# Sooner loads and a new order of scores in a windowed-attention and ReGLU kernel

## The chip, the cores and the metric

The kernel runs on one core of one Trainium2 chip. The metric is device time in microseconds, as the median of several executions, each kernel beside executions of the kernel before on the same chip in the same rounds. The profile of a kernel is one traced execution; its span, from the first to the last instruction of the core, is 1.7 to 1.8 us shorter than the device time of the same execution.

## The reference

Attention over q, k, v of shape (4, 8, 768, 64), in which a row sees the first 4 positions and its last 128; the output, as 3072 rows of 512, goes through a gated feed-forward layer.

```python
keep = is_sink | in_window                 # n_sink = 4, window = 128
a = softmax(where(keep, q @ k.T / sqrt(64), -1e9))
x = (a @ v).transpose(0, 2, 1, 3).reshape(3072, 512)
out = (maximum(x @ w_gate, 0) * (x @ w_val)) @ w_out      # d_ff = 1536
```

## The kernel before

Attention works in 16 units: unit i is one pair of heads of batch i // 4, so the "first four pairs" are batch 0. The feed-forward work is cut into 96 chunks, each half a batch (384 rows) by 128 of the 1536 columns. Units 0 to 3 and the first three stages of unit 4 run first; after them the stages of attention are put between chunks by a plan.

A unit's k, q and v are loaded from DRAM into f32 staging (four buffers in turn) by the SP queue. GpSimd casts them to bf16 and issues the weight loads on its own queue. In batches 0 and 1 TensorE transposes q and k (`T`); in batches 2 and 3 a DMA on the SP queue does (`X`). VectorE then copies strips of kT into kTs (`sinkk`).

```python
def X(self):                      # batches 2 and 3: two transposes by DMA, on the SP queue
    for x, dst in ((self.kn, kT[self.s]), (self.qn, qT[self.s])):
        nc.sync.dma_start_transpose(...)

def held(x):                      # a load that waits for VectorE to reach this memset
    if x < len(U):
        nc.vector.memset(U[x].stg[0:1, 0:1], 0.0)
        load(x)                   # k, q, v0, v1 on nc.sync; vt too for a batch's first unit

def unit_stages(x):
    u, prev, nxt = U[x], at(x - 1), at(x + 1)
    def s(gi):                    # scores of group gi, then exp on ScalarE
        def f():
            # ... cut
            if gi == 0 and nxt is not None and nxt.xbar:
                nxt.X()
            u.S(gi)
        return f
    def v():                      # second outputs of the unit before, and their normalisation
        if prev is not None:
            norm(prev, 1, ps_at if on_array else ps_gv)
    def t():                      # next unit's T and kTs, then loads, casts, weights
        # ... cut: nxt.T(...), nxt.sinkk()
        if x == 3:
            load(6)
        elif x == 4:
            load(7)
        elif x >= 5:
            held(x + 3)
        # ... cut: load_wo at x = 4 and 5; casts(at(x + 3), "kqv"); load_w at x = 0, 1, 3, 4
        if x == 0:
            load(5)
    # ... cut: v0 is norm(u, 0)
    if x < NP:
        return [s(0), v, s(1), t, s(2), v0]

def chunk(b, c0, n, m):           # cut to its operations
    gp = x @ wg[:, m]             # four matmuls on TensorE, PSUM pool of three buffers
    gs = relu(gp)                 # ScalarE
    vp = x @ wv[:, m]             # four matmuls, same pool
    hT[:, m] = gs * vp            # VectorE
PLAN = ((0, 28), (24, 50), (48, 62), (71, 74))    # (chunk, stages to be out by then)
```

The softmax here doesn't subtract the row's maximum and nothing guards it: scores larger than these inputs give would overflow.

## Time and profile before

| | before |
|---|---|
| device time | 260.46 us (259.57 to 260.71, 3 runs) |
| span of the traced run | 258.7 us |
| TensorE busy | 249.4 us, 96% |
| TensorE's last long wait | 1.97 us, for hT, to 75.87 |
| span from there to the end | 182.8 us |

Most lines behind it are in the prediction below; the one on which TensorE resumes is

```profile
75.87 0.81 PE L290 MATMUL gp<-xT,wg 128*128 128x384 bf16 x4 [1.97 <-DVE hT L298]
```

A timeline line is start, duration, engine, source line, operation, output <- inputs, shapes, count; the bracket tells how long the engine stood idle before it and what ended that.

### The profile page before, as it was taken

The numbers are of one execution on the slowest core, as the hardware profiler recorded it, in microseconds if no ns is written. First come the engines' busy times: TensorE is split into PE (matmuls) and PEld (weight loads), VectorE is DVE, ScalarE is ACT, GpSimd is POOL, SyncE is SP. The second block draws the span as 40 slices with busy tenths as digits, with TensorE's granted clock in tenths as the row PEclk, the third lists the DMA queues.
The fourth block names the chain that finished last, engine by engine and source line by source line (L and its number), as shares of the span: only waits on it lengthen the run. The fifth ranks groups of instructions, "written<-read, shape, count | busy, mean of one in ns | idle before, by whom it ended". The sixth has DMA issues, their size and how long they took to land.

```text
span 258.7 us, 5201 instructions
## 1 busy us (share of the span) xinstructions
PE 249.4 (96%) x2046; PEld 143.5 (55%) x2046; DVE 144.5 (56%) x313; ACT 115.6 (45%) x188; POOL 62.3 (24%) x94
## 2 busy tenths in 40 slices
PE   7999799999969999999999999999999999999994
PEld 7565466565545555546555555556555555555443
DVE  2598869886748564756656665756664322322100
ACT  3887665647424444443535344344533332333212
POOL 6779538801535221404040210000000000000000
PEclk9999999999999999999999999999999999999999
DMA  7999999999989948869491961311011101111132
GB/s 213 309 279 253 246 257 197 196 198 199 218 125 239 197 111 157 129 145 138 85 242 43 184 104 42 61 43 41 3 41 41 42 1 41 43 41 41 41 112 94
DMA packets 77320, 33.56 MB, mean 130 GB/s; under 512 B 64368, under 2 KB 74352, under 8 KB 77296
## 3 DMA queue, kind: packets, MB, share of 16 engines
q1 hardware_dynamic: 69920, 28.12, 48.5%
q0 software_dynamic: 5808, 4.72, 12.1%
q10 hardware_dynamic: 1568, 0.39, 0.7%
q8 instruction: 16, 0.26, 0.5%
q14 instruction: 8, 0.07, 0.1%
HBM read 28.51 MB, written 6.29 MB: 135 GB/s over the span
## 4 chain that ended last, share of the span: by engine, by line
PE 68%; DMA 13%; SPq 8%; POOL 6%; issue 2%; DVE 1%; ACT 0%; POOLq 0%; DVEq 0%; ACTq 0%
PE op L310 23%; PE gp L290 19%; PE vp L296 18%; DMA stg<-in_v_dram 11%; PE ops L206 5%; SPq L119 4%; PE sps L181 3%; SPq L114 2%; DMA kT<-kn 2%; POOL vn L129 2%; SPq L111 1%; SPq L331 1%; POOL kn L126 1%; POOL vn L130 1%; POOL wg L225 1%
## 5 line engine op out<-in xcount | busy, mean ns | idle before, releaser
L298 DVE TENSOR_TENSOR hT<-gs,vp 128x384 bf16<-128x384 f32 x96 | 52.8, 550 | 54.4 <-PE vp L296 52.7
L290 PE MATMUL gp<-xT,wg 128*128 128x384 bf16 x384 | 78.5, 327 | 2.0 <-DVE hT L298 2.0
L296 PE MATMUL vp<-xT,wv 128*128 128x384 bf16 x384 | 78.1, 326 | 1.1 <-DMA wv<-in_moe_w_val_dram 1.1
L293 ACT ACTIVATE gs<-gp 128x384 f32<-128x384 f32 x96 | 47.1, 490 | 61.5 <-PE gp L290 60.3
L310 PE MATMUL op<-wo,hT 128*128 128x512 bf16 (+1 forms) x300 | 74.4, 370 | 0.0
L185 ACT ACTIVATE ee<-sps 128x1006 bf16<-128x1006 f32 (+2 forms) x48 | 46.1, 966 | 46.9 <-PE sps L181 46.8
L296 PEld LDWEIGHTS <-wv 128*128 128x128 bf16 x384 | 37.5, 98 | 26.2 <-DMA wv<-in_moe_w_val_dram 1.5
L290 PEld LDWEIGHTS <-wg 128*128 128x128 bf16 x384 | 34.0, 98 | 31.8 <-issue 6.7
L310 PEld LDWEIGHTS <-hT 128*128 128x128 bf16 x300 | 29.4, 98 | 25.0
L187 DVE TENSOR_TENSOR ee<-ee,msk 128x1006 bf16<-128x1006 bf16 (+2 forms) x36 | 25.1, 698 | 11.3 <-ACT ee L185 11.3
L126 POOL CAST kn<-stg 128x768 bf16<-128x768 f32 x15 | 13.2, 879 | 59.0 <-DMA stg<-in_k_dram 39.6
L314 ACT COPY ot<-op 128x512 f32<-128x512 f32 (+1 forms) x25 | 14.2, 569 | 24.5 <-PE op L310 24.5
L275 DVE STREAM_TRANSPOSE R<-ops 128x384 f32<-128x384 f32 x24 | 13.9, 581 | 12.6 <-PE ops L206 12.5
L278 DVE STREAM_TRANSPOSE R<-rc 128x384 f32<-128x384 f32 x32 | 18.5, 578 | 1.1
L280 DVE TENSOR_TENSOR xT<-ops,R 128x384 bf16<-128x384 f32 x32 | 17.8, 557 | 1.7
L206 PEld LDWEIGHTS <-ones 128*64 128x64 bf16 x288 | 12.3, 109 | 11.2 <-issue 10.8
L129 POOL CAST vn<-stg 128x768 bf16<-128x768 f32 x16 | 13.3, 832 | 15.0 <-DMA stg<-in_v_dram 15.0
L126 POOL CAST qn<-stg 128x768 bf16<-128x768 f32 x15 | 13.3, 888 | 11.9 <-DMA stg<-in_q_dram 7.1
L206 PE MATMUL ops<-ee,vn 128*64 128x255 bf16 (+7 forms) x256 | 15.3, 240 | 0.2 <-DVE xT L280 0.2
L181 PE MATMUL sps<-qT,kT 64*128 64x251 bf16 (+2 forms) x128 | 14.7, 252 | 0.5 <-ACT qT L154 0.4
L181 PEld LDWEIGHTS <-kT 64*128 64x128 bf16 x128 | 6.3, 93 | 12.9 <-issue 10.5
L181 PE MATMUL sps<-qT,kTs 64*128 64x248 bf16 (+1 forms) x96 | 12.3, 253 | 0.0
(57 smaller groups left out, 135.5 us busy)
## 6 DMA issues: line engine op xcount, KB each, us to landing
stg<-in_k_dram SPq DMA_DIRECT2D x16, 384.0 KB, 4.9
stg<-in_q_dram SPq DMA_DIRECT2D x16, 384.0 KB, 5.4
out_dram<-ot SPq DMA_DIRECT2D x23, 256.0 KB, 2.0
stg<-in_v_dram SPq DMA_DIRECT2D x30, 192.0 KB, 5.4
wg<-in_moe_w_gate_dram POOLq DMA_DIRECT2D x4, 384.0 KB, 7.7
wv<-in_moe_w_val_dram POOLq DMA_DIRECT2D x4, 384.0 KB, 9.8
wo<-in_moe_w_out_dram POOLq DMA_DIRECT2D x3, 512.0 KB, 13.6
stg<-in_v_dram ACTq DMA_DIRECT2D x2, 192.0 KB, 6.4
```

The source lines that it names most:

```text
L126: cp((self.kn if what == "k" else self.qn)[:], self.staging(what).rearrange("p h (n d) -> p n h d", d=64))
L129: eng.tensor_copy(self.vn[:], self.staging("v"))
L181: nc.tensor.matmul(out=ps[:, h, c:c + w], lhsT=self.kw(j, r), rhs=qT[s][r, qa:qa + w], start=not self.biased, stop=True, skip_group_check= ...
L185: nc.scalar.activation(x, ps[:, :, 0:c], Act.Exp, bias=0.0, scale=scale)
L187: nc.vector.tensor_tensor(x, x, bc(msk[:, m0:m0 + c], 2), op=Alu.mult)
L206: nc.tensor.matmul(out=ps[1 - what][64 * h:64 * h + 64, qa - q0:qa - q0 + w], lhsT=self.vw(j, h) if what else ones[:], rhs=ee[s][:, gi, h, ...
L278: nc.vector.transpose(r[:, 1, 0:w], bass.AP(a.tensor, a.offset, [a.ap[0], [1, nb], [0, 32]]))
L290: nc.tensor.matmul(out=gp[:, 0:n], lhsT=wg[:, ko, m * 128:(m + 1) * 128], rhs=x[:, ko, c0:c0 + n], start=ko == 0, stop=ko == KO - 1)
L293: nc.scalar.activation(gs[:, 0:n], gp[:, 0:n], Act.Relu, bias=0.0, scale=1.0)
L296: nc.tensor.matmul(out=vp[:, 0:n], lhsT=wv[:, ko, m * 128:(m + 1) * 128], rhs=x[:, ko, c0:c0 + n], start=ko == 0, stop=ko == KO - 1)
L298: nc.vector.tensor_tensor(hT[:, m, c0:c0 + n], gs[:, 0:n], vp[:, 0:n], op=Alu.mult)
L310: nc.tensor.matmul(out=op, lhsT=hTs[b][:, m, t * 128:(t + 1) * 128], rhs=wo[:, m, c0:c0 + n], start=m == 0, stop=m == FM - 1)
```

## The change

The intent: ScalarE should get its second scores sooner in the first four pairs; loads of later batches should start sooner and fill a gap of the DMA engines at 42 to 47 us. (The change's description also speaks of moving w_out ahead; no line of the diff does that.)

```diff
-                if x == 3:
+                if x == 2:
+                    held(5)
+                elif x == 3:
                     load(6)
                 elif x == 4:
                     load(7)
-                elif x >= 5:
-                    held(x + 3)
+                if x >= 4:
+                    held(x + 4)
...
-                if x == 0:
-                    load(5)
...
             if x < NP:
-                return [s(0), v, s(1), t, s(2), v0]
+                return [s(0), s(1), v, t, s(2), v0]
...
-        PLAN = ((0, 28), (24, 50), (48, 62), (71, 74))
+        PLAN = ((0, 28), (6, 32), (24, 50), (48, 62), (71, 74))
```

## The prediction

> **What bounds the kernel now.** I read the page first, then who made TensorE wait, then the timeline round the largest wait, then the DMA queue's own timeline and the packets of each queue by stretch.
>
> The page: busy TensorE, the 40 slices of PE and of DMA (a slice is 6.5 us).
>
> ```profile
> PE 249.4 (96%) x2046; PEld 143.5 (55%) x2046; DVE 144.5 (56%) x313; ACT 115.6 (45%) x188; POOL 62.3 (24%) x94
> PE   7999799999969999999999999999999999999994
> DMA  7999999999989948869491961311011101111132
> ```
>
> TensorE is the bound: after its dip in slice 11 (71 to 78 us) it never stops. But the DMA engines are full for the first 71 us too, and the dips of PE lie there. TensorE's waits by releaser (us in total, times, longest):
>
> ```profile
> PE gp L290 <- DVE hT L298: 2.0, 1, 2.0
> PE vp L296 <- DMA wv<-in_moe_w_val_dram: 1.1, 1, 1.1
> ```
>
> The 2.0 us wait is at 73.9 to 75.87. VectorE's timeline there:
>
> ```profile
> 69.40 0.54 DVE L298 TENSOR_TENSOR hT<-gs,vp 128x384 bf16<-128x384 f32 x1
> 74.87 0.41 DVE L161 COPY kTs<-kT 128x372 bf16<-128x372 bf16 x1 [4.93 <-DMA kT<-kn]
> 75.27 0.54 DVE L298 TENSOR_TENSOR hT<-gs,vp 128x384 bf16<-128x384 f32 x1
> ```
>
> VectorE stands 4.93 us at kTs of unit 8 (batch 2's first pair, first to be transposed by DMA); the hT products behind it wait too, PSUM fills, and TensorE stops 2.0 us. TensorE resumes 1.0 us after kT lands (74.84 to 75.87). From there it has no stop but the tail, so the end time is: landing of unit 8's kT, plus 1.0, plus 182.8 of span (258.66 - 75.87).
>
> Why it lands at 74.8, from the DMA queue's timeline (start, time the queue's sequencer was held):
>
> ```profile
> 39.18 0.60 SPq L331 DMA_DIRECT2D vt<-in_v_dram  x1
> 47.18 0.37 SPq L111 DMA_DIRECT2D stg<-in_k_dram  x1
> 47.65 3.26 SPq L111 DMA_DIRECT2D stg<-in_q_dram  x1
> 51.01 12.26 SPq L119 DMA_DIRECT2D stg<-in_v_dram  x2
> 63.35 2.67 SPq L111 DMA_DIRECT2D stg<-in_k_dram  x1
> 66.12 1.25 SPq L111 DMA_DIRECT2D stg<-in_q_dram  x1
> 67.46 2.21 SPq L119 DMA_DIRECT2D stg<-in_v_dram  x2
> 69.84 1.62 SPq L135 DMA_TRANSPOSE kT<-kn  x1
> ```
>
> Unit 8's loads go out at 47.18 (held until then by a VectorE memset), unit 9's at 63.35, and only behind them, in program order, unit 8's transpose. The v loads hold the queue 12 us. Packets of the two queues in 50 to 65 us (first two lines) and of the load queue alone in 66 to 71 us:
>
> ```profile
> q0 software_dynamic: 2365, 2.08, 85.8%
> q1 hardware_dynamic: 3400, 0.86, 36.9%
> ```
> ```profile
> q1 hardware_dynamic: 4153, 1.05, 97.3%
> ```
>
> q0 is the weights, q1 all loads, transposes and stores of the SP queue. With both at work q1 gets 3400/15 = 227 packets per us and q0 2365/15 = 158; alone, q1 gets 4153/5 = 830. And in 42 to 47, where unit 8's loads are held back (last columns: DMA share, GB/s):
>
> ```profile
> 42.00:47.00 5.00, 5.00 (x45) 2.94 (x44) 4.79 (x10) 3.51 (x6) 5.00 (x7) 1.00 0.99 120
> 50.00:65.00 15.00, 15.00 (x137) 8.61 (x137) 11.56 (x25) 9.00 (x15) 1.86 (x2) 1.00 1.23 197
> ```
>
> That gap is what sooner loads can use.
>
> [...] in 58 to 64 us the two queues moved 927 and 925 packets, one for one, and unit 8's transpose ran only behind unit 9's loads. [...] batch 2's loads are 256 B pieces, and they ran at 210 GB/s in 66 to 71 us against 330 in 38 to 40, where unit 7's k and q came in rows of 384 f32, 1536 B. [...]
>
> **The change part by part.**
>
> (1) Order in the first four pairs. Now TensorE runs first scores, previous pair's second outputs, second scores. ScalarE waits 0.84 us per pair for the second scores (25 us: exp at 24.93), and the outputs wait some 0.3 us for the third exp. Putting scores first feeds ScalarE earlier and removes both. But the normalisation of those outputs then starts later, and the pair's own outputs need its PSUM buffer (three in that pool). VectorE needs about 2.1 us (24.11 to 26.22). The new loop is normalisation 2.1 + outputs 0.4 + two biased scores 0.85 each + sums 0.35 + hand-overs 0.35 = 4.9 us, and the pairs now take 4.9 (first scores at 21.98 and about 26.9). So nothing in the middle pairs; at the end of the stage about 0.5 us, for unit 4's scores no longer wait for qT. Then the first vp waits for wv anyway. An earlier TensorE before 70 us is in any case eaten by the wait at 74.
>
> (2) Unit 5's load moves from pair 0 to pair 2, behind a memset: its k goes out at about 22.3, not 19.39. The first weights, issued at 21.25, lose a competitor: perhaps 0.8 us off the 1.1 us wait. The load queue runs dry for about 1.2 us, some of which the weights use; I carry +0.6 us to everything behind it.
>
> (3) Loads 8 and later go out one unit sooner. Unit 8's k then follows vt directly (about 40 us). But the order on the SP queue, which I compared instruction for instruction, becomes loads 8, 9, 10, then transpose 8; before it was 8, 9, transpose 8. A unit is 128x12 + 128x12 + 2 x 128x6 = 4608 packets (check: 43 to 72 us has 9443, two units and vt). So q1 must move 13824 packets before the transpose instead of 9216. It starts at 43, not at about 50. q0's 3696 packets of 43 to 72 us take 3696/158 = 23.4 us beside it, to 66.4; q1 moves 23.4 x 227 = 5310 meanwhile; the other 8514 take 8514/830 = 10.3 us: unit 10's last packet at about 76.7. Unit 9's was at about 72.0 before (by counting). That is +4.7. The weights alone reached 215 per us in 44 to 50 (1287 in 6) only after a slow start, so q1 can take more at first: -0.8. With (2): 4.7 - 0.8 + 0.6 = +4.5 us on kT's landing, 79.3, and TensorE resumes at 80.4.
>
> (4) The added point in the plan moves stages by at most one chunk between chunks 3 and 10: nothing. The diff holds no line that moves w_out; POOL's order is unchanged, and w_out now competes with unit 8. It should land about 1 us later (before: at most 66 us; first used after 70), no wait.
>
> Later units keep their distances: load x+4 is followed by transpose x+2 as load x+3 by x+2 before, and the profile shows no wait for a transpose after the first. No new wait there. One 59 ns memset more.
>
> Sum: 260.46 + 4.5 = 265.0. I put in a fifth of a chance that the order on the queue costs less than I think, and say 264.5.
>
> **Rivals.** (a) The intended one: the loads were only late, the gap of 42 to 47 is used, unit 8 lands before 70, both waits go: 260.5 - 2.0 - up to 0.8 = about 258. For it: 120 GB/s in that gap, 4.9 us of waiting. Against it: unit 8's loads need not be the limit, the transpose's place behind a third unit is. (b) Mine: 262.5 to 267. (c) DMA work only changes places: the gap's extra packets (7 us x 227 = 1590) pay a third of the added 4608, and the rest is small if q1 beside q0 runs faster than 227; at 400 the landing moves by about +2: 262.5. (d) The weights suffer: w2 is issued at 42.03 and used at about 52.9; its 1024 packets at 158 take 6.5 us, so it lands near 51 to 52. A wait of 1 us there would be swallowed by the one at 74.
>
> **Range and chances.** Faster by over 2% means under 255.3, less than any removed wait allows: 3%. The 2% line upward is 265.7, inside my spread of 262.5 to 267.5: 37%. Within 2%: 60%. The range, 259 to 267.5, leaves (a) just outside.
>
> **What would show it.** Right: on the SP queue the transpose of unit 8 after three loads, at about 74; VectorE's wait at kTs of some 9 us ending near 79; TensorE's one wait for hT there of 6 to 7 us; the first vp's wait smaller; no gap at 42 to 47. Wrong: kTs without a wait and transpose 8 out before 68 (then (a)), or TensorE waiting for wg or wv of the later weight parts, or a wait after 90 us.

## More of the kernel before

All runs quoted here are of the state called fast.

One row of the page the prediction doesn't show will matter: the clock that was granted to TensorE, in tenths (9 is full) for 40 slices of the span.

```profile
PEclk9999999999999999999999999999999999999999
```

It is full all along in this execution. Such a row is easily passed over where nothing stands in it. It is not full in every execution of this kernel: in 11 of the 36 that ran beside the experiments the mean granted clock was 0.986 to 0.993. A mean of 0.993 stands for some 3.6 us at half clock, an estimate (0.007 x 259 us, doubled).

## The result, and the profile after

The changed kernel took 267.62 us (266.37 to 268.27, 4 runs) where the kernel before took 260.58 (259.57 to 261.67, 4 runs): ratio 1.0263, 95% interval 1.0207 to 1.0320. A second measurement later, on another chip, gave 265.78 (265.39 to 266.85, 6 runs) and 1.0202 (1.0162 to 1.0242). A ratio is the mean time of one kernel's fast runs over that of the other's fast runs of the same rounds, so not quite the ratio of the medians. So it is slower by about 5 to 7 us, on or a little over the 2% line.

TensorE's waits in the changed kernel (total, times, longest, in us):

```profile
PE gp L290 <- DVE hT L298: 5.6, 1, 5.6
PE vp L296 <- DMA wv<-in_moe_w_val_dram: 2.8, 2, 1.5
```

The one wait for hT has grown from 2.0 to 5.6 us, and there are two waits for wv. The SP queue's timeline:

```profile
41.09 1.47 SPq L111 DMA_DIRECT2D stg<-in_k_dram  x1
...
52.44 4.18 SPq L111 DMA_DIRECT2D stg<-in_k_dram  x1
...
70.94 0.59 SPq L111 DMA_DIRECT2D stg<-in_k_dram  x1
71.61 1.33 SPq L111 DMA_DIRECT2D stg<-in_q_dram  x1
73.03 3.34 SPq L119 DMA_DIRECT2D stg<-in_v_dram  x2
76.55 1.58 SPq L135 DMA_TRANSPOSE kT<-kn  x1
```

The three k loads are those of units 8, 9 and 10; the transpose is unit 8's. Unit 8's load went out at 41.09 (47.18 before), but its transpose at 76.55 (69.84 before), since unit 10's load stands ahead of it. VectorE pays with 8.94 us in place of 4.93:

```profile
80.20 0.29 DVE L161 COPY kTs<-kT 128x372 bf16<-128x372 bf16 x1 [8.94 <-DMA kT<-kn]
80.41 0.15 DVE L162 COPY kTs<-kT 128x12 bf16<-128x12 bf16 x1
80.48 0.54 DVE L298 TENSOR_TENSOR hT<-gs,vp 128x384 bf16<-128x384 f32 x1
```

and TensorE resumes at 81.08 (75.87 before):

```profile
72.61 0.82 PE L290 MATMUL gp<-xT,wg 128*128 128x384 bf16 x4
...
81.08 1.44 PE L290 MATMUL gp<-xT,wg 128*128 128x384 bf16 x4 [5.64 <-DVE hT L298]
82.31 1.48 PE L296 MATMUL vp<-xT,wv 128*128 128x384 bf16 x4
```

Here is the second thing, which the prediction did not have: the same four matmuls take 0.82 us before the wait and 1.44 behind it. The page's clock row dips, and TensorE by stretch (start:end, length, busy us of PE, PEld, DVE, ACT and POOL with counts, then granted clock, DMA share, GB/s) shows half clock:

```profile
PEclk9999999999995999999999999999999999999999
```
```profile
80.00:82.00 2.00, 0.92 (x4) 0.41 (x4) 1.80 (x7) 0.00 (x0) 0.86 (x2) 0.53 0.38 79
82.00:84.00 2.00, 2.00 (x7) 0.88 (x6) 1.90 (x5) 0.49 (x1) 0.00 (x0) 0.50 1.14 256
84.00:86.00 2.00, 2.00 (x19) 1.06 (x19) 0.46 (x1) 0.00 (x0) 0.82 (x1) 0.50 1.32 220
86.00:88.00 2.00, 2.00 (x21) 1.08 (x15) 1.31 (x3) 0.88 (x1) 0.83 (x1) 0.76 1.40 152
```

TensorE reads as fully busy from 82 on (2.00 of 2.00 us at a granted clock of 0.50). The busy share does not show the slow clock here; only the durations and the clock column do. The trace's clock records put the half-clock stretch at 80.13 to 86.95, 6.83 us.

In the traces every half-clock stretch inside the kernels lasted 3.41 or 6.83 us, and it stood beside a wait of TensorE (5.64 us of waiting and 6.83 us at half clock here). How long a wait brings it is taken up under b_only2 and in the last section.

So the traced span, 7.8 us longer (266.5 - 258.7), comes apart into two terms: the resume is 5.2 us later (81.08 - 75.87), and from the resume to the end it took 2.6 us more (185.4 against 182.8).

### The profile page after: what moved, and what is told of

It is laid out like the page before. It is cut to its first block, busy times and chain, and to the rows that moved or that the text cites. A ratio compares the mean times of both kernels' runs of the same rounds, so it can differ in the third digit from the quotient of the medians.

```text
span 266.5 us, 5185 instructions
## 1 busy us (share of the span) xinstructions
PE 250.6 (94%) x2023; PEld 144.2 (54%) x2046; DVE 145.2 (54%) x314; ACT 115.9 (43%) x188; POOL 61.7 (23%) x94
## 4 chain that ended last, share of the span: by engine, by line
PE 73%; DMA 15%; POOL 4%; SPq 4%; issue 2%; ACT 1%; DVE 0%; POOLq 0%; ACTq 0%; DVEq 0%
PE op L310 23%; PE gp L290 21%; PE vp L296 20%; DMA stg<-in_v_dram 7%; PE ops L206 6%; DMA wv<-in_moe_w_val_dram 4%; PE sps L181 3%; DMA stg<-in_k_dram 3%; SPq L114 2%; DMA kT<-kn 1%; SPq L119 1%; SPq L331 1%; POOL vn L129 1%; POOL kn L126 1%; POOL wg L225 1%
## 5 line engine op out<-in xcount | busy, mean ns | idle before, releaser
L290 PE MATMUL gp<-xT,wg 128*128 128x384 bf16 x384 | 79.1, 329 | 6.0 <-DVE hT L298 5.6
L310 PE MATMUL op<-wo,hT 128*128 128x512 bf16 (+1 forms) x277 | 71.3, 373 | 1.2
L187 DVE TENSOR_TENSOR ee<-ee,msk 128x1006 bf16<-128x1006 bf16 (+2 forms) x36 | 25.8, 716 | 11.0 <-ACT ee L185 11.0
L129 POOL CAST vn<-stg 128x768 bf16<-128x768 f32 x16 | 13.9, 871 | 33.5 <-PE ops L206 13.7
L126 POOL CAST kn<-stg 128x768 bf16<-128x768 f32 x15 | 12.5, 831 | 34.9 <-issue 18.8
L126 POOL CAST qn<-stg 128x768 bf16<-128x768 f32 x15 | 12.5, 831 | 14.0 <-DMA stg<-in_q_dram 13.8
L161 DVE COPY kTs<-kT 128x372 bf16<-128x372 bf16 x16 | 6.8, 424 | 14.0 <-DMA kT<-kn 8.9
```

Of the source, the lines that this page charges most:

```text
L126: cp((self.kn if what == "k" else self.qn)[:], self.staging(what).rearrange("p h (n d) -> p n h d", d=64))
L187: nc.vector.tensor_tensor(x, x, bc(msk[:, m0:m0 + c], 2), op=Alu.mult)
L290: nc.tensor.matmul(out=gp[:, 0:n], lhsT=wg[:, ko, m * 128:(m + 1) * 128], rhs=x[:, ko, c0:c0 + n], start=ko == 0, stop=ko == KO - 1)
L310: nc.tensor.matmul(out=op, lhsT=hTs[b][:, m, t * 128:(t + 1) * 128], rhs=wo[:, m, c0:c0 + n], start=m == 0, stop=m == FM - 1)
```

## The experiments

Twelve runs were made: ten kernels, one of them twice, and the changed kernel once more. The theories: A, that the place of unit 8's transposes behind unit 10's loads on the SP queue makes the kernel slower; and D, that the long wait costs a second time through TensorE's clock. Their rivals are that the sooner loads as such (traffic), the score order or the later load of unit 5 cost it, and that the clock is a by-product that costs nothing.

What the traces showed, one traced run each. "Issued" is unit 8's first transpose on the SP queue, "kTs" VectorE's copy behind it, "resume" TensorE's start after its wait for hT. For ratios see the text.

| kernel | median us | issued | kTs | resume | span | span - resume | half clock behind the resume |
|---|---|---|---|---|---|---|---|
| before | 260.46 | 69.84 | 74.87 | 75.87 | 258.7 | 182.8 | none |
| after | 267.62 | 76.55 | 80.20 | 81.08 | 266.5 | 185.4 | to 86.95 |
| after_again | 265.78 | 75.14 | 78.55 | 79.44 | 263.9 | 184.4 | to 83.02 |
| a_order | 260.72 | 69.41 | 73.07 | no wait | 257.7 | | none |
| a_undo3 | 260.66 | 70.41 | 75.78 | 76.65 | 259.4 | 182.8 | none |
| b_only3 | 265.70 | 74.35 | 79.11 | 79.99 | 264.2 | 184.2 | to 83.18 |
| a_busy | 265.50 | 76.27 | 79.53 | 80.75 | 263.5 | 182.8 | none |
| a_busy_again | 265.62 | 75.39 | 78.64 | 79.52 | 262.3 | 182.8 | none |
| b_only1 | 260.75 | 69.84 | 75.13 | 76.01 | 258.8 | 182.8 | none |
| b_only2 | 262.09 | 71.02 | 75.14 | 76.02 | 260.3 | 184.3 | 76.99 to 80.41 |
| best2 | 260.83 | 60.77 | 70.56 | no wait | 257.4 | | none |
| best3 | 259.71 | 61.37 | 71.16 | no wait | 258.0 | | none |
| a_wo_later | 260.64 | 63.84 | 72.17 | no wait | 258.3 | | none |
| b_transpose_first | 260.64 | 65.35 | 72.04 | no wait | 258.9 | | none |

The column "span - resume" is the one to read: 182.8 in the five traces with full clock there, and 1.4 to 2.6 more in each of the four with half clock behind the resume.

### a_order: the changed kernel, with unit 10's and later loads behind the transposes

```diff
                     if gi == 0 and nxt is not None and nxt.xbar:
                         nxt.X()
+                        held(x + 3)
...
-                if x >= 4:
+                if x in (4, 5):
                     held(x + 4)
```

> The changed kernel, but each load from unit 10 on is issued just behind the transposes of the unit two before it, so the order on the load queue is 8, 9, transposes of 8, 10, as before the change. Theory A (the place of unit 8's transposes behind a third unit sets when kT lands): kT lands near 75 instead of 80.2, TensorE waits at most 2 us for hT, no clock drop, time 259.5 to 261.5. Theory B (the sooner loads and the weights slow each other, the order hardly matters): kT still lands at 79 or later, time 265 or more.

Measured: 260.72 us (259.47 to 262.03, 4 runs), 0.9962 of the kernel before (0.9900 to 1.0024). Its SP queue:

```profile
65.73 3.51 SPq L119 DMA_DIRECT2D stg<-in_v_dram  x2
69.41 1.57 SPq L135 DMA_TRANSPOSE kT<-kn  x1
71.09 1.22 SPq L135 DMA_TRANSPOSE qT<-qn  x1
72.41 0.53 SPq L111 DMA_DIRECT2D stg<-in_k_dram  x1
```

Unit 8's transpose goes out 7.1 us sooner than in the changed kernel, kTs waits 1.4 us, TensorE has no wait for hT near 75 us, and the clock is full in the traced run. All other parts of the change stand. The whole loss is gone with this one order: A holds. That it does not beat the kernel before clearly, though it lost a wait of 2.0 us, is taken up below.

### a_undo3: the changed kernel without the sooner loads of units 8 and later

```diff
-                if x >= 4:
-                    held(x + 4)
+                if x >= 5:
+                    held(x + 3)
```

> The changed kernel with the sooner loads of units 8 and later undone (unit x+3 again at unit x), all else changed. Theory A: near the kernel before, 259.5 to 261.5; what unit 5's later load costs (I put +0.6 us on the landing) is inside that. A theory C, that unit 5's late load or the new order of the scores carries the loss: 265 or more.

Measured: 260.66 us (259.88 to 261.49, 4 runs), 0.9953 (0.9890 to 1.0015). The resume is at 76.65, at the place of before. The other parts of the change cost nothing that can be seen.

### b_only3: the kernel before with the sooner loads alone

```diff
-                elif x >= 5:
-                    held(x + 3)
+                if x >= 4:
+                    held(x + 4)
```

> The kernel before with the sooner loads of units 8 and later alone. Theory A: all of the loss or nearly, 266 to 268, with kTs of unit 8 at 79 to 80.5 and a TensorE wait of 5 us or more there. Theory C: 260 to 262.

Measured: 265.70 us (264.68 to 268.42, 4 runs), 1.0168 (1.0094 to 1.0242). Three of the four runs had a mean clock of 0.981 to 0.987.

```profile
79.99 1.44 PE L290 MATMUL gp<-xT,wg 128*128 128x384 bf16 x4 [3.38 <-DVE hT L298]
```

The direction is as expected, the time a little under the 266 expected at least, and the wait of TensorE 3.4 us and not 5. The resume is nevertheless 4.1 us later than before (79.99 - 75.87): TensorE came to the wait later, for it had waited 1.9 us for wv at 32.25 and 0.7 for wg. So the resume, and not the length of the wait, is the measure of the loss. With a_undo3, this part makes the loss and the others don't.

### a_busy: the changed kernel with 96 multiplications inside the wait

TensorE multiplies the identity by itself into unused columns of the PSUM tile of unit 7's first outputs, just before it would wait. The result is unchanged and correct. If theory D holds, the clock stays up.

```diff
         o, sums = u.V(part, pool)
+        if u.i == 7 and part == 0:
+            for _ in range(96):
+                nc.tensor.matmul(out=sums[:, 384:512], lhsT=ident[:], rhs=ident[:], start=True, stop=True,
+                                 skip_group_check=True)
```

> The changed kernel with 96 matmuls of 128 columns of the identity into an unused corner of PSUM, placed just ahead of TensorE's wait at 75 us, some 5.3 us of work in what was an idle wait of 5.6 us. The landing of kT should not move. Theory D (after the long idle wait the granted clock fell to 0.5 for some 6 us, which costs 2 to 3 us on top of the wait): the clock stays at 1.0, time 265 to 265.8, 1.5 to 3 us less than the changed kernel. If the clock is not the cause, or costs nothing on the path: within 0.5 us of the changed kernel's 267.6.

Measured: 265.50 us (265.07 to 266.11, 4 runs), 1.0146 (1.0095 to 1.0197), against 267.62 and 1.0263 of the changed kernel, which had been measured earlier and elsewhere. I took the 2.1 us for the clock's.

### after_again and a_busy_again: both in the same rounds

No edit: the changed kernel, and the one with the 96 multiplications.

> The changed kernel unchanged, in the same rounds as the one with the 96 multiplications in its wait, to size the clock term beside it. Theory (landing plus clock): about 267.5 us (266.3 to 268.5), mean granted clock .981 to .987, ratio to the kernel before 1.022 to 1.03; a stretch of 3.4 or 6.8 us at half clock just behind the wait for hT at 75 to 81 us. Rival (the first measurement's excess over the kernel with 96 multiplications was chance or another chip): both within 0.8 us of each other.

> The kernel with 96 multiplications of the identity in the wait, a second time. Theory: 265.0 to 266.0 us at a granted clock of .993 to 1.0, thus 1.4 to 2.6 us under the changed kernel in the same rounds, with the transposed kT landing as late (79 to 80 us) as there. Rival: no difference of more than 0.8 us.

Measured: the changed kernel 265.78 us (265.39 to 266.85, 6 runs; mean clock 0.987 to 0.994), ratio 1.0202 (1.0162 to 1.0242); the other 265.62 us (263.83 to 266.96, 6 runs; mean clock 0.992 to 1.0), ratio 1.0176 (1.0131 to 1.0221). That is 0.2 us between the medians and 0.6 between the means: by the times, the rival's outcome, and the 2.1 us above was not the clock's alone.

The device times hide something, though. In every execution of every other kernel the device time is 1.73 to 1.84 us longer than the span; in the ten executions with the multiplications it is 1.77 to 2.90 us longer. So the multiplications add up to 1.1 us outside the span, and why is not known. By the spans of the same rounds the changed kernel takes 264.2 us on average (263.6 to 265.1) and the one with the multiplications 263.2 (261.8 to 264.1), 1.1 us less.

The traces say what they said before. The changed kernel:

```profile
79.44 1.44 PE L290 MATMUL gp<-xT,wg 128*128 128x384 bf16 x4 [5.41 <-DVE hT L298]
80.67 1.48 PE L296 MATMUL vp<-xT,wv 128*128 128x384 bf16 x4
```

and with the multiplications:

```profile
73.54 5.53 PE L275 MATMUL ops<-ident 128*128 128x128 bf16 x96
79.52 0.81 PE L294 MATMUL gp<-xT,wg 128*128 128x384 bf16 x4 [0.44 <-DVE hT L302]
80.17 0.81 PE L300 MATMUL vp<-xT,wv 128*128 128x384 bf16 x4
```

Both resume within 0.1 us of each other (kTs at 78.55 and 78.64), the first then runs at half clock until 83.02, and its span is 1.6 us longer (263.9 against 262.3), all of it behind the resume. So half clock costs 1.6 us in one traced run and 2.6 in another. That the medians show so little of it is in part the time outside the span. Two more causes may add to it, and these runs don't tell them apart: the landing of kT varies between executions, and only one of each kernel is traced, the quickest but one of its six for a_busy_again; and the multiplications are themselves a floor, for they end at about 79.1, so that an earlier landing would bring that kernel nothing. The clock's term is shown in the traces. Its mean over executions stays rough: 1.1 us by the spans, whose ranges overlap, and 0.6 by the device times.

A second thing that the repetition tells: kT's landing itself is not fixed. In the first trace of the changed kernel the DMA engines stood nearly idle from about 69 to 71 us, ahead of unit 10's k (a share of 0.23 and 48 GB/s), in the second they did not (158 to 258 GB/s), and the transpose went out 1.4 us sooner (75.14). What caused that gap I haven't found.

### b_only1: the kernel before with the score order and the plan alone

```diff
-                return [s(0), v, s(1), t, s(2), v0]
+                return [s(0), s(1), v, t, s(2), v0]
...
-        PLAN = ((0, 28), (24, 50), (48, 62), (71, 74))
+        PLAN = ((0, 28), (6, 32), (24, 50), (48, 62), (71, 74))
```

> The kernel before with the new order of the scores in the first four pairs and the new plan alone. Prediction's step 1: the pairs' pace of 4.9 us stays, the first chunk starts some 0.3 to 0.5 us sooner, but its second product waits for wv until about 31 as before, and what is gained is eaten by the wait at kTs of unit 8: within 0.5% of before. A rival: the freed waits of ScalarE and TensorE pay: 1 us or more faster.

Measured: 260.75 us (259.31 to 261.77, 4 runs), 1.0006 (0.9940 to 1.0073). No gain and no loss, as expected. The sooner first chunk did not come: in the traced run it began at 29.53 (29.14 before), and its second product, after waits of 1.1 us for wg and 1.9 for wv, at 32.22 (31.07 before). Yet TensorE resumed at 76.01 (75.87 before): the wait near 75 us swallowed this late start.

### b_only2: the kernel before with the later load of unit 5 alone

```diff
-                if x == 3:
+                if x == 2:
+                    held(5)
+                elif x == 3:
                     load(6)
...
-                if x == 0:
-                    load(5)
```

> The kernel before with unit 5's load moved to pair 2 behind the memset, alone. Prediction's step 2: wv some 0.8 us sooner at the first chunk, kT of unit 8 some 0.6 us later, time within 0.5% of before. What the changed kernel's trace suggests instead: the weight queue moves at the same rate without its competitor (498 packets in 22 to 26 us against 466), so wv's landing stays within 0.3 us of 31.0.

Measured: 262.09 us (261.15 to 262.24, 4 runs), 1.0053 (1.0007 to 1.0100). The first vp started at 31.23 after 1.23 us of waiting for wv (31.07 after 1.10 before), so the weights came no sooner. The transpose went out at 71.02, 1.2 us later, but kTs only 0.3 later (75.14). Three of the four runs had a mean clock of 0.993, and in the trace half clock for 3.41 us costs 1.5 us. The small loss agrees with that term in size (the kernel before had a mean clock under 0.998 in none of its seven runs of these rounds); it is at the edge of what can be told from noise.

Why did a wait of 1.95 us bring half clock here, and one of 1.97 none in the trace of before? The clock records of each trace begin at some time (5.84 us in the trace of before, 5.31 here), and every change of the clock behind it lies a multiple of 3.413 us later. Counted in such windows, the wait of before is cut in two by an edge at 74.11, and the wait here lies in one window whole. First the window of before, then the two here (start:end, length, busy us of PE, clock, DMA share, GB/s):

```profile
74.11:77.52 3.41, 1.65 (x10) 1.00 0.51 115
73.58:76.99 3.41, 1.46 (x23) 1.00 0.52 98
76.99:80.41 3.42, 3.42 (x26) 0.50 1.25 242
```

In the fourteen traces all nine windows at full clock with less than 1.5 us of busy TensorE were followed by half clock (0.00 us in 76.72 to 80.13 of the changed kernel, 1.46 here; the last windows of a kernel are counted, as 0.37 us in 255.01 to 258.42 of the kernel before). Of those with more, one was (a_undo3, 1.62 us of 28.09 to 31.50); two with 1.55 (b_only1) and 1.59 us (best2) and all with 1.65 us or more were not. So in these traces a window about half idle was enough (1.46 us busy of 3.41), and of two waits of like length the one that lay in one window whole (1.95 us) brought half clock and the one cut in two (1.97 us) did not; busy times are modelled, so the border is rough.

### best2: transposes ahead of the next unit's loads, unit 8 loaded sooner, score order

An attempt to beat both. From unit 8 on, the next unit's load follows the transposes of this one, and casts move with the loads. Based on the kernel before:

```diff
                         nxt.X()
+                        held(x + 2)
...
-                elif x >= 5:
-                    held(x + 3)
+                if x == 4:
+                    held(8)
...
-                if at(x + 3) is not None:
-                    casts(at(x + 3), "kqv")
+                y = x + 3 if x < 6 else x + 2
+                if at(y) is not None and x != 6:
+                    casts(at(y), "kqv")      # and cast_t for y, as before
...
-                return [s(0), v, s(1), t, s(2), v0]
+                return [s(0), s(1), v, t, s(2), v0]
```

> A candidate: the kernel before with the new order of the scores, unit 8's load one unit sooner, and the load of each later unit behind the transposes of the unit before it, so the order on the queue is 8, transposes of 8, 9, transposes of 9, 10. Theory A: transposes of 8 go out at about 61 to 63, where kT's buffer comes free, and land by 70, so neither VectorE nor TensorE waits for them; the clock stays at 1.0 there; 257.5 to 259.5. If the weights hold back the load queue so much that kT lands at 73 or later even so: 260 or more.

Measured: 260.83 us (259.22 to 261.83, 4 runs), 1.0007 (0.9949 to 1.0064). The mechanism is there: transpose at 60.77, kTs at 70.56 without a wait for a transfer, no wait for hT. The median missed. In the traced run (259.22 us) TensorE reached the first vp at 31.99 (31.07 before) behind waits for kTs, xT and wv; three of the four runs had a mean clock of 0.991 to 0.993.

### best3: best2 with the first weights issued ahead of unit 3's casts

```diff
+                if x == 0:
+                    load_w(0)
...
-                if x in (0, 1, 3, 4):
+                if x in (1, 3, 4):
```

> The candidate best2, with the first weight part issued ahead of unit 3's casts instead of behind them, about 3.5 us sooner. If nothing else suffers, wv is there before the first chunk wants it, its wait of 1.1 us and any half clock after it go: 1 to 2.5 us less than best2. If the loads of unit 4, beside which it now runs, come late, the fourth pair waits instead and nothing is gained.

Measured: 259.71 us (259.49 to 260.97, 4 runs), 0.9979 (0.9930 to 1.0028). The wait for wv is gone (first vp at 30.53), the clock is 0.999 or 1.0 in all runs, but GpSimd's casts, now behind the weight issues, made a new wait of 1.24 us at 34.11. It is the lowest median of all, and not told apart from the kernel before.

### a_wo_later: a_order with two parts of w_out one unit later

```diff
-                if 4 <= x < 6:
-                    for c in ((0,), (1, 2))[x - 4]:
+                if x in (4, 6):
+                    for c in ((0,), (), (1, 2))[x - 4]:
```

> The changed kernel with loads 10 and later behind the transposes of the unit two before (which ran at 260.7), and w_out's parts 1 and 2 issued one unit later. Theory: with fewer weight packets beside the loads of units 8 and 9 these end sooner, the transposes of unit 8 go out at 66 to 69 us instead of 69.4, VectorE no longer waits at kTs, TensorE doesn't wait for hT near 75 us; 259.0 to 260.8 us, ratio .992 to 1.0. Rival (weights only move, the total of packets before 70 us is the same or w_out itself comes late at its first use after 70 us): 260.5 to 262 with a wait for wo.

Measured: 260.64 us (260.04 to 261.15, 6 runs), 0.9992 (0.9958 to 1.0026). The transpose went out at 63.84, 5.6 us sooner than in a_order, as expected and sooner. But kTs still waited 2.2 us to 72.17: the issue came 5.6 us sooner and the landing 0.9, presumably because both parts of w_out were issued at 64.19 and ran beside the transpose. And the rival's wait came too:

```profile
77.33 0.38 PE L310 MATMUL op<-wo,hT 128*128 128x512 bf16 x1 [1.35 <-DMA wo<-in_moe_w_out_dram]
```

A wait went and another of 1.35 us took its place; no gain.

### b_transpose_first: the kernel before with the transposes ahead of the next unit's loads, and nothing else

The edit is best2's without the score order and with `held(8)` left at x == 5.

> The kernel before with one thing changed: from unit 8 on a unit's two transposes go out ahead of the next unit's loads (the order on the queue is loads 8, transposes 8, loads 9, transposes 9, loads 10), and unit 9's and later casts move one unit later with the loads; the loads of unit 8 stay where they are. Theory (what stands ahead of the transposes sets the resume at 75.9): transposes of 8 issued at 62 to 66 us, kTs without a wait on a transfer, no wait of TensorE for hT near 75 us; the wait for wv at 31 us stays at 1.1; 258.0 to 259.6 us, ratio .990 to .997, clock 1.0. Rival (loads of 9 then land later and unit 9's casts or transposes make a new wait near 78 to 84 us): 260 to 262 us with that wait in the trace.

Measured: 260.64 us (258.55 to 261.39, 6 runs) against 261.05 (11 runs), 0.9954 (0.9907 to 1.0001). TensorE has no wait for hT, as expected, nor a new wait later. The median missed the expected 259.6 by 1.0. The traced run (260.71) shows where the gain went: TensorE began its first chunk at 32.17, and at 29.14 in the trace of before, although both kernels have the same instructions in the same order up to there on every engine but the SP queue's later part. Two of VectorE's copies into kTs were slow that had been quicker before. Before, with the time and then the duration:

```profile
16.78 0.54 DVE L161 COPY kTs<-kT 128x372 bf16<-128x372 bf16 x1
21.75 0.40 DVE L161 COPY kTs<-kT 128x372 bf16<-128x372 bf16 x1 [0.31 <-ACT kT L154]
```

and in this run:

```profile
17.39 1.26 DVE L161 COPY kTs<-kT 128x372 bf16<-128x372 bf16 x1
22.69 1.27 DVE L161 COPY kTs<-kT 128x372 bf16<-128x372 bf16 x1
```

GpSimd cast kn at 17.69 to 18.51 and at 22.95 to 23.81 there, inside both copies, and both copies ended 0.14 to 0.15 us after the cast (18.65 and 23.96). This is no single case: of the 224 such copies in the fourteen traces, 60 took over 0.30 us, all 60 beside a cast, a copy or a weight issue of GpSimd, and 38 of them ended 0.13 to 0.16 us after a GpSimd instruction. The trace of before has one too, 1.29 us at 11.45. (31 of the 164 quick copies also ran beside such work.) So I take GpSimd's work beside them for what slows these copies; but no run here takes the casts away, so this cause is argued from the times and not shown by an experiment.

What is shown is that the first chunk starts anywhere from 28.9 to 32.2 us in these traces, and why a removed wait of 2.0 us brings so little. In the three traces whose first vp is followed by no long wait of TensorE (a_order, best2, b_transpose_first) the time from the first vp to the end is 225.4 to 225.7 us, and in the trace of before 227.6, its wait of 2.0 included. So the wait is saved; but b_transpose_first's first vp came at 33.25 (31.07 before), and that took the gain back. In the kernel before, the wait swallows such late starts, as b_only1 showed; the kernels without it pay them in full.

## Why the prediction was right or wrong

The prediction said 264.5 us; 267.62 was measured first, 0.1 above the top of the range (267.3, and inside it, when the ratio is put on the prediction's own 260.46), and 265.78 the second time, within it. The larger part of its chances, 60%, lay on "within 2%", and the ratios are 1.026 and 1.020. Direction and mechanism were right; the size was short by 3.1 and 1.3 us.

Step (3), the queue. Right in the order, and in part lucky in its sum. Three loads stand ahead of the transpose. The landing said to be at 79.3 is that of kTs at 80.2, 78.6, 79.5 and 78.6 in the four traces with the changed queue and score order, 79.2 on average. The two rates it was built of held as means: in 44 to 67 us of the changed kernel the load queue moved 5431 packets, 236 per us (227 used), and the weight queue 3657, 159 per us (158 used). They are not the rates of the two side by side. In 44 to 50 us the load queue moved 2475 packets beside 753 of the weights, and in 50 to 62 us 2077 beside 2144, so 173 per us and one for one. The 227 is such a mean too. The issue "at about 74" was 75.1 to 76.6, later than said, and from there to kTs it took 3.25 to 3.65 us (5.03 before, and 5.3 by the prediction's two times); the two errors largely cancel in the landing. a_order undoes exactly this step and the loss goes.

"From there it has no stop but the tail", with 182.8 of span: this is the step that failed, in the sum 260.46 + 4.5. The 182.8 is right at full clock, to a tenth, in all five traces that have such a wait and full clock. But in the traces in which TensorE stood for 3.4 to 5.6 us it came back at half clock, and in the two traces of the changed kernel the stretch took 185.4 and 184.4. The term is about 0.45 of the time in which half clock overlaps with work: 2.6 of 5.9 us, 1.6 of 3.6, 1.4 of 3.2 and 1.5 of 3.4 in the four traces. The resume itself was 5.2 us later in the first trace and 3.6 in the second, where 4.5 was said. The prediction counted 6 to 7 us of waiting (5.6 and 5.4 measured) and had no term for the clock behind it. The discount of 0.5 us for doubt went the wrong way too.

Step (1), the score order. Right in that nothing comes of it. b_only1 is at 1.0006. In the changed kernel TensorE's transposes of the pairs are at 14.90, 19.66 and 24.55 (14.89, 19.86 and 24.76 before): the pace of 4.9 us stays within 0.2, and the first chunk came 0.3 us sooner (28.86; in b_only1 0.4 later), of which nothing reached the end.

Step (2), unit 5's load. The 0.8 us off the wait for wv did not come: TensorE waited 1.48 us to 31.15 (1.10 to 31.07 before). The step took the weight queue to be slowed by the load queue at its start. Packets in 22 to 26 us, before and then after:

```profile
q0 software_dynamic: 466, 0.35, 67.2%
q1 hardware_dynamic: 755, 0.57, 46.0%
```
```profile
q0 software_dynamic: 498, 0.38, 84.0%
q1 hardware_dynamic: 372, 0.10, 11.5%
```

The competitor moved half as many packets and the weight queue 7% more. It is slow at its start by itself: in 23.5 to 25.5 us it moved 351 packets in the changed kernel, where the load queue moved none, and 353 before, beside 100. And the competitor was moved, not removed: in 26 to 30 us the load queue carried 0.81 MB (0.52 before) and the weight queue 458 packets (579 before). So wg landed 5.1 us after its issue (6.7 before), but wv 8.8 (8.9 before). The later wait swallowed the 0.1 us. The +0.6 us for what stands behind it is not shown: b_only2's kTs is 0.3 later.

Step (4). No effect of the plan was found, as said. w_out made no wait in the changed kernel.

Rivals. (a), 258, is out as long as the transposes stand behind unit 10; with the order mended, traced spans do lie at 257.4 to 258.9, but the medians at 259.7 to 260.8. (c), 262.5, is out: the load queue moved 236 packets per us beside the weights on average and not 400, although it did so (412) in the first 6 us. Its sum is also wrong by the prediction's own numbers: at 400 per us, 9360 packets go by 66.4 and the other 4464 by 71.8, so that the landing does not move; +2 us belongs to some 320 per us. (d) came and was swallowed as said: a wait of 1.29 us for wv, ending at 54.19. A wait for a later weight part stood on the prediction's list of signs that it is wrong; it came and meant nothing for the time.

## What to carry to other kernels

Before loads are moved ahead on a queue, look at what stands behind them that is wanted sooner: here the SP queue issued in program order, and loads 6 us sooner became a kT that lands 4 to 5 us later, and putting one load behind the transposes gave it all back. A wait is measured by when the bounding engine resumes, and its cost doesn't end there: where TensorE stands for some microseconds, read the clock and the durations behind it (here, behind 5.64 us, a clock of 0.50 and 1.44 us for four matmuls instead of 0.82). And a wait that several late starts hide in is worth less when it is removed than its length says.

## What the traces show of the clock, the queues and the copies

- Into half clock: a window about half idle was enough. With 1.46 us of busy TensorE in it (b_only2, a wait of 1.95 us, ended at 76.02) half clock followed, with 1.65 us (before, a wait of 1.97 us) it did not, and between them it went either way (1.62 in a_undo3 did; 1.55 and 1.59 in b_only1 and best2 did not).
- Out of half clock: a window with 2.46 of 3.41 us busy did not end it in the changed kernel (80.13 to 83.54), one with 3.19 did in b_only3 (79.77 to 83.18).
- What half clock cost: 1.4 to 2.6 us in stretches of 3.41 to 6.83 us, a quarter to 0.43 of their length, because part of a stretch can lie in the wait itself; of the 3.2 to 5.9 us that overlapped with work it is about 0.45.
- In two stretches the weight queue and the load queue moved packets one for one (1383 and 1373 in 54 to 62 us before, 2144 and 2077 in 50 to 62 us of the changed kernel), together 345 and 352 packets per us. In 44 to 50 us of the changed kernel it was 753 and 2475.
- The weight queue, issued by GpSimd, at its start: 351 packets in 23.5 to 25.5 us with nothing of the load queue beside it, 353 with 100.
- A VectorE copy of 128x372 took 0.28 to 0.30 us in 164 of 224 cases. The other 60 were longer (1.29 us at 11.45 in the trace of before, 1.27 at 22.69 in b_transpose_first), all beside work of GpSimd, if that is the cause.
